# A PSUM bank for slot 7 and a place for the sixth pair of output tiles, in a fused sliding-window attention and MLP kernel

## The chip, the cores and the metric

The kernel runs on one core of one Trainium2 chip. The metric is the device time of one execution in microseconds, as the median of several executions. One program computes both stages; it holds most of its intermediate values on the chip and writes only the final output to memory.

## The reference, cut to what matters

Attention with a window of 32 positions to either side, on 8 batches of 8 heads, 576 positions and 64 elements per head. Its output, laid out as 4608 tokens of 512 elements, goes through a two-layer product with the piecewise quadratic activation SMeLU between the layers.

```python
def _attn_ref(q, k, v):                      # (8, 8, 576, 64) each
    scores = scale * np.matmul(q, k.transpose(0, 1, 3, 2))
    mask = np.abs(pos[:, None] - pos[None, :]) <= window      # window = 32
    scores = np.where(mask, scores, -1000000000.0)
    ...                                      # softmax over the last axis
    return np.matmul(attn, v)

def _moe_ref(x, w_in, w_out):                # x (4608, 512), w_in (512, 2048), w_out (2048, 512)
    h = x @ w_in
    g = np.where(h >= 1, h, np.where(h <= -1, 0.0, (h + 1) ** 2 / 4))
    return g @ w_out
```

## The kernel before, in the parts that matter

The second stage sets the rhythm. The tokens are taken in 18 blocks of 256 (TB), the hidden width of 2048 in 8 parts of 256 (NF). One *slot* `a` computes one part of one block: `t, f = divmod(a, 8)`. Slots 0 to 7 are block 0, slots 8 to 15 block 1, and so on. A slot does the following, in this order on each engine (the order of the text is the order of the instructions, engine by engine[...]):

```python
    for a in range(NF * NB + NF):
        t, f = divmod(a, NF)
        eng = None if a < 14 else V
        post = [x for n, x in pairs if n == a] + [a - NF] * (a >= 2 * NF + 2)
        # ... loads
        if a == 0 or a > 3:
            flush()                          # VectorE: xT <- attention output (L305, L308)
        if t < NB:
            # ... gT[t]
            r0 = TB * t % RING
            if a in (6, 7):
                hp = ps_o.tile([128, 2, TB], FP, name="hp", tag="op")
            else:
                hp = ps_h.tile([128, 2, TB], FP, name="hp", tag="hp")
            for j in range(2):
                for n, kk in enumerate((0, 2, 1, 3)):
                    nc.tensor.matmul(hp[:, j], w_in[:, kk, ...], xT[:, kk, r0:r0 + TB],   # L492, 8 of them
                                     start=n == 0, stop=n == 3)
            rr = ewp.tile([128, 2, TB], FP, name="rr")
            A.activation(rr, hp, AF.Relu, scale=0.5, bias=0.5)                           # L496
            g = gT[t][:, 2 * f:2 * f + 2]
            mx = ewp.tile([128, 2, TB], FP, name="mx")
            if a in two_on_act:              # (1, 7, 8, 9, 10, 11, 12)
                A.activation(mx, rr, AF.Square)                                          # L500
                V.scalar_tensor_tensor(g, hp, 1.0, mx, op0=ALU.max, op1=ALU.min)         # L501, reads hp
            else:
                V.tensor_max(mx, hp, rr)                                                 # L503, reads hp
                V.scalar_tensor_tensor(g, rr, 1.0, mx, op0=ALU.min, op1=ALU.mult)        # L504
        flush()
        run(a)                               # attention work placed at slot a
        for x in post:
            (pair if x < 4 * 4 else quarter)(x)      # second product: L448 in a pair, L432 in a quarter
        run(a + 0.5)                         # attention work placed after the second product
        # ... transposing loads
```

PSUM pools: `ps_h` gives the tiles `hp`, one bank each, and has two of them; `ps_o` gives the output tiles `op`, one bank each, and has two as well. A pool hands its banks out in turn, and a matmul that starts a new tile waits until the readers of the tile before it in that bank are done.

```python
    ps_h = ctx.enter_context(tc.tile_pool(name="ps_h", bufs=2, space=bass.MemoryType.PSUM))
    # ... ps_s and ps_n: one tile of two banks each, for scores, sums and transposes
    ps_o = ctx.enter_context(tc.tile_pool(name="ps_o", bufs=2, space=bass.MemoryType.PSUM))
```

In `ps_o` the order of tiles is: two small score tiles (slot 2), `hp` of slot 6, the output tile of block 0's first half (pairs 0 to 3), `hp` of slot 7, the output tile of block 1's first half (pairs 4 to 7), and then output tiles alone.

A *pair* is a quarter of the second product of one block for one half of the output columns, eight matmuls; it needs four parts of `gT` and half of the columns of four row blocks of `w_out`:

```python
    pairs = [(6, 0), (8, 1), (9, 2), (10, 3), (11, 4), (13, 5), (15, 6), (15, 8), (16, 7), (17, 9)]   # (slot, pair)

    def pair(x):
        half, p, g = x // 8, x % 8 // 4, x % 4       # half of the columns, block, group of four j
        # ... op[half, p] from ps_o at its first use
        for tt in range(2):
            for j in range(4 * g, 4 * g + 4):
                nc.tensor.matmul(o[:, tt], gT[p][:, j, ...], w_out[:, j, 256 * half:256 * half + 256], ...)   # L448
        # ... after the fourth: A.copy(osb, o) and a store of 256 rows
```

The attention work that stands near by:

```python
    at(3, (scores, 0, (1, 2), (0, 2), (2, 4), ps_n), (sums, 0, 0, TB, MAIN, ps_s))
    at(4, (sums, 0, 1, TB, MAIN))
    at(5, (sums, 0, 0, MAIN, S, ps_s))               # the last part of batch 0's attention, for slot 8's xT
    at(11, (tposes, 1, (0, 0), (0, 1)))              # batch 1: q transposed on TensorE (L187), copied to qT (L190)
    at(12, (tposes, 1, (1, 0), (1, 1)))              # batch 1: k likewise, to kT; written in the source as a loop
    at(13, seq[0][1])                                # batch 1: scores (bias L206, product L227, exp L235)
    at(13.5, (*seq[1][1], ps_n))                     # batch 1: scores, second part
    at(14, (*seq[0][0], ps_s), seq[1][0])            # batch 1: sums (L293), for slot 16's xT
```

Of the kernel before, what the change touches and what calls it, by code (L numbers as in the profile page):

```python
# [14 lines left out]
def kernel(  # L15
# [78 lines left out]
    def load_nat(b, t):  # L94
        src, dst, nm = ((q, qn, "qn"), (k, kn, "kn"))[t]
        x = dst[b] = nat.tile([128, NU, 2, D], BF, name=nm, tag=nm)
        for h in range(2):
            nc.gpsimd.dma_start(out=x[:, :, h], in_=src[b, NY * h:NY * h + NY].rearrange("y s d -> (y s) d")  # L98
                                .rearrange("(u p) d -> p u d", p=128))

    def load_v(b, n):
        if b not in vn:
            vn[b] = nat.tile([128, 2 * NC, 2, D], BF, name="vn", tag="vn", bufs=3)
        h, a = divmod(n, 2)
        y = NY * h + 2 * a
        nc.gpsimd.dma_start(out=vn[b][64 * a:64 * a + 64, :, h], in_=v[b, y:y + 2].rearrange("y s d -> (y s) d")  # L106
                            .rearrange("(c r) d -> r c d", r=64))
# [84 lines left out]
    def xpose(b, t):  # L192

        nc.sync.dma_start_transpose(out=qkT(b, t).rearrange("d (u p) -> d u p", p=128),
                                    in_=(qn, kn)[t][b].rearrange("p u h d -> p (u h d)"))
# [115 lines left out]
    def flush():  # L311
        while muls:
            muls.pop(0)()
# [61 lines left out]

    NB = NT // TB
    NF = DFF // 256
    pairs = [(6, 0), (8, 1), (9, 2), (10, 3), (11, 4), (13, 5), (15, 6), (15, 8), (16, 7), (17, 9)]
    two_on_act = (1, 7, 8, 9, 10, 11, 12)
    ev = {}  # L380

# [34 lines left out]
    for b in range(LONG, B):  # L416
        a = sl[5 * (b - 1) - 7] - 17
# [39 lines left out]
    def run(pos):  # L457
        todo = []
        for fn, *x in ev.get(pos, []):
            if fn is sums:  # L460
                todo.append(sums(*x))
            elif fn is tposes:
                tposes(*x)
            else:
                pool = (x.pop(),) if x[-1] in (ps_s, ps_n, ps_o) else ()
                fn(*x, eng, *pool)
        for end in todo:
            end()
# [5 lines that stand above are left out]
        for b, x in loads.get(a, []):  # L474
            if x < 2:
                load_nat(b, x)
            else:
                for n in range(4):
                    load_v(b, n)
# [3 lines that stand above are left out]
            if t not in gT:  # L483
                gT[t] = gtp.tile([128, 2 * NF, TB], BF, name="gT", tag="gT")
            r0 = TB * t % RING
            if a in (6, 7):
                hp = ps_o.tile([128, 2, TB], FP, name="hp", tag="op")
            else:
                hp = ps_h.tile([128, 2, TB], FP, name="hp", tag="hp")
            for j in range(2):  # L490
                for n, kk in enumerate((0, 2, 1, 3)):
                    nc.tensor.matmul(hp[:, j], w_in[:, kk, 256 * f + 128 * j:256 * f + 128 * j + 128],  # L492
                                     xT[:, kk, r0:r0 + TB], start=n == 0, stop=n == 3)
# [5 lines that stand above are left out]
            if a in two_on_act:  # L499
                A.activation(mx, rr, AF.Square)  # L500
                V.scalar_tensor_tensor(g, hp, 1.0, mx, op0=ALU.max, op1=ALU.min)  # L501
            else:
                V.tensor_max(mx, hp, rr)  # L503
                V.scalar_tensor_tensor(g, rr, 1.0, mx, op0=ALU.min, op1=ALU.mult)  # L504
        flush()
        run(a)
        for x in post:
            (pair if x < 4 * 4 else quarter)(x)
        run(a + 0.5)
        for x in xps.get(a, []):  # L510
            xpose(*x)
# [30 lines left out]
```

The softmax here doesn't subtract the row's maximum and nothing guards it: scores larger than these inputs give would overflow.

## Time and profile before

| | |
|---|---|
| time, median of 3 executions | 313.86 us (313.83 to 314.38) |
| the profiled execution | 313.74 us, of which 311.6 us are the span from the first to the last instruction |
| TensorE (PE) busy | 297.6 us, 95% of the span |
| VectorE (DVE) busy | 244.9 us, 79% |
| ScalarE (ACT) busy | 195.3 us, 63% |
| software DMA queue (GpSimd's loads) | 75.5% of the time of 16 DMA engines |

How to read it. Every instruction of the trace has a start in microseconds from the span's start, a duration, and, where its engine sat idle before it, the length of that idle time and the instruction that ended it (the releaser). The views used here are the page's first and fourth parts (busy time by engine; the chain of work that ended last), the list of waits of one engine, and the timeline of one engine in a window. A timeline merges equal instructions that follow each other and puts their number behind an x; the second column is then the time from the first one's start to the last one's end. Successive matmuls overlap, so the ends of neighbouring rows overlap too; the distance between two starts tells what one group costs. In the timeline of TensorE, L492 is a slot's first product, L448 a pair, L187 a transpose, L206 and L227 the bias and the product of a score tile, L293 the sums of attention and L432 a quarter of the second product for one tile of 128 tokens.

### The profile page before, as it was taken

How to read it: one execution, taken by the hardware profiler on the slowest of the kernel's cores; microseconds unless marked ns; L12 is line 12 of the kernel's file. 1: busy time of each engine (PE TensorE's matmuls, PEld its weight loads, DVE VectorE, ACT ScalarE, POOL GpSimd, SP SyncE). 2: the span in 40 equal slices, each digit the busy share in tenths (PEclk: the TensorE clock that was granted, in tenths of full speed). 3: DMA queues.
4: the chain of work that ended last, by engine and by line, in shares of the span. 5: the costliest groups of instructions: out<-in, count | busy, mean ns of one | idle time of the engine just before them, and what ended most of it. 6: DMA issues, size and time to landing. Idle time of an engine off the chain costs nothing.

```text
span 311.6 us, 8569 instructions
## 1 busy us (share of the span) xinstructions
PE 297.6 (95%) x3669; PEld 207.2 (66%) x3706; DVE 244.9 (79%) x381; ACT 195.3 (63%) x323; POOL 73.5 (24%) x89
## 2 busy tenths in 40 slices
PE   8997989999999999999999999999999999999995
PEld 3566868886666666666666666666666666666652
DVE  4287558888888888888888888888888888888760
ACT  3686876776765766567656666566676666554431
POOL 8898344643061223040504000000000000000000
PEclk9999999999999999999999999999999999999999
DMA  9999999999999999597998592005501100110111
GB/s 151 183 198 199 175 214 177 173 164 167 168 176 131 112 187 162 62 112 153 160 95 81 65 154 70 34 36 113 111 34 36 37 34 36 37 36 34 52 51 67
DMA packets 124118, 34.54 MB, mean 111 GB/s; under 512 B 108208, under 2 KB 119728, under 8 KB 124080
## 3 DMA queue, kind: packets, MB, share of 16 engines
q0 software_dynamic: 94736, 18.06, 75.5%
q1 hardware_dynamic: 29200, 15.63, 20.9%
q8 instruction: 29, 0.48, 0.6%
q10 hardware_dynamic: 144, 0.29, 0.3%
q14 instruction: 9, 0.07, 0.1%
HBM read 36.70 MB, written 9.44 MB: 148 GB/s over the span
## 4 chain that ended last, share of the span: by engine, by line
PE 91%; DVE 3%; ACT 3%; issue 3%; ACTq 0%
PE hp L492 39%; PE op L432 35%; PE bb L293 6%; PE op L448 4%; PE bb L227 2%; PE z L336 2%; PE tp L187 1%; DVE kT L190 1%; DVE xT L305 1%; ACT rc L300 1%; DVE mx L503 1%; ACT rr L496 1%; ACT lr L299 1%; DVE gT L501 0%; ACT mx L500 0%
## 5 line engine op out<-in xcount | busy, mean ns | idle before, releaser
L492 PE MATMUL hp<-xT,w_in 128*128 128x256 bf16 x1152 | 149.3, 273 | 2.8 <-DVE mx L503 1.9
L496 ACT ACTIVATE rr<-hp 128x512 f32<-128x512 f32 x144 | 85.7, 595 | 88.3 <-PE hp L492 88.2
L492 PEld LDWEIGHTS <-w_in 128*128 128x128 bf16 x1152 | 111.9, 98 | 42.5 <-issue 3.3
L432 PE MATMUL op<-w_out,gT 128*128 128x512 bf16 x477 | 123.0, 379 | 5.1 <-issue 4.9
L503 DVE TENSOR_TENSOR mx<-hp,rr 128x512 f32<-128x512 f32 x137 | 94.5, 690 | 31.8 <-ACT rr L496 29.6
L504 DVE SCALAR_TENSOR_TENSOR gT<-rr,mx 128x512 bf16<-128x512 f32 x137 | 95.3, 696 | 4.7
L432 PEld LDWEIGHTS <-gT 128*128 128x128 bf16 x512 | 47.5, 98 | 36.8
L235 ACT ACTIVATE pt<-bb 128x1024 bf16<-128x1024 f32 (+1 forms) x33 | 32.8, 1002 | 5.3 <-PE bb L227 3.8
L106 POOL DMA_DIRECT2D vn<-in_v_dram x32 | 27.3, 868 | 34.1 <-PE bb L227 31.5
L305 DVE TENSOR_TENSOR xT<-bb,rc 128x512 bf16<-128x512 f32 (+1 forms) x32 | 21.1, 658 | 10.1 <-ACT rc L300 9.6
L437 ACT COPY osb<-op 128x512 f32<-128x512 f32 x32 | 18.6, 583 | 11.5 <-PE op L432 11.1
L300 ACT ACTIVATE rc<-lr 128x512 f32<-128x512 f32 (+2 forms) x40 | 23.5, 587 | 1.3
L98 POOL DMA_DIRECT2D qn<-in_q_dram x10 | 12.2, 1221 | 43.5 <-DMA qT<-qn 37.5
L299 ACT ACTIVATE lr<-bb 128x512 f32<-128x512 f32 (+2 forms) x40 | 22.0, 551 | 0.2 <-PE bb L293 0.2
L201 DVE TENSOR_TENSOR pt<-pt,mask 128x1024 bf16<-128x1024 bf16 (+1 forms) x33 | 20.3, 614 | 0.0
L293 PE MATMUL bb<-pt,ones 64*64 64x256 bf16 (+3 forms) x352 | 19.5, 255 | 0.1
L293 PE MATMUL bb<-pt,vn 64*64 64x128 bf16 (+3 forms) x712 | 18.4, 204 | 0.0
L293 PEld LDWEIGHTS <-vn 64*64 64x64 bf16 x712 | 16.7, 107 | 0.2 <-DMA vn<-in_v_dram 0.2
L448 PE MATMUL op<-w_out,gT 128*128 128x256 bf16 x128 | 16.5, 273 | 0.0
L293 PEld LDWEIGHTS <-ones 64*64 64x64 bf16 x352 | 10.2, 105 | 8.5 <-issue 8.4
L98 POOL DMA_DIRECT2D kn<-in_k_dram x10 | 12.1, 1213 | 10.7 <-DMA kT<-kn 3.9
L227 PE MATMUL bb<-qT,kT 64*64 64x128 bf16 (+1 forms) x520 | 13.1, 217 | 0.4 <-DVE kT L190 0.4
(56 smaller groups left out, 118.7 us busy)
## 6 DMA issues: line engine op xcount, KB each, us to landing
out_dram<-osb SPq DMA_DIRECT2D x36, 256.0 KB, 2.3
vn<-in_v_dram POOLq DMA_DIRECT2D x32, 144.0 KB, 8.8
qn<-in_q_dram POOLq DMA_DIRECT2D x10, 288.0 KB, 7.2
kn<-in_k_dram POOLq DMA_DIRECT2D x10, 288.0 KB, 8.0
w_in<-in_moe_w_in_dram POOLq DMA_DIRECT2D x12, 128.0 KB, 5.6
w_out<-in_moe_w_out_dram POOLq DMA_DIRECT2D x3, 512.0 KB, 15.5
qn<-in_q_dram POOLq DMA_DIRECT2D x2, 576.0 KB, 12.8
kn<-in_k_dram POOLq DMA_DIRECT2D x2, 576.0 KB, 13.9
```

The costliest lines, as they stand in the source:

```text
L98: nc.gpsimd.dma_start(out=x[:, :, h], in_=src[b, NY * h:NY * h + NY].rearrange("y s d -> (y s) d") .rearrange("(u p) d -> p u d", p=128))
L106: nc.gpsimd.dma_start(out=vn[b][64 * a:64 * a + 64, :, h], in_=v[b, y:y + 2].rearrange("y s d -> (y s) d") .rearrange("(c r) d -> r c d", ...
L235: A.activation(p, ps[:, :, :w * n].rearrange(like, y=m), AF.Exp, scale=D ** -0.5)
L293: nc.tensor.matmul(bb[HD[h], a, o + c0:o + c1], ones[HD[a]] if c is None else vn[b][HD[a], c, h], p(a, h), start=n == 0, stop=True, skip_g ...
L299: A.activation(lr[:, :, :D0], bb[:, :, D0:2 * D0], AF.Ln)
L300: A.activation(rc[:, :, :D0], lr[:, :, :D0], AF.Exp, scale=-1.0)
L432: nc.tensor.matmul(o, gT[tt // 2][:, j, 128 * (tt % 2):128 * (tt % 2) + 128], w_out[:, j], start=not done, stop=len(done) == 2 * NF - 1, s ...
L448: nc.tensor.matmul(o[:, tt], gT[p][:, j, 128 * tt:128 * tt + 128], w_out[:, j, 256 * half:256 * half + 256], start=not done, stop=len(done ...
L492: nc.tensor.matmul(hp[:, j], w_in[:, kk, 256 * f + 128 * j:256 * f + 128 * j + 128], xT[:, kk, r0:r0 + TB], start=n == 0, stop=n == 3)
L496: A.activation(rr, hp, AF.Relu, scale=0.5, bias=0.5)
L503: V.tensor_max(mx, hp, rr)
L504: V.scalar_tensor_tensor(g, rr, 1.0, mx, op0=ALU.min, op1=ALU.mult)
```

## The change

Two edits. Slot 7's `hp` is taken from `ps_h` as in most slots, and only slot 6's comes from `ps_o`. Pair 5 (block 1, first half of the columns, parts 2 and 3 of block 1's `gT`, made in slots 10 and 11) is done in slot 12, after that slot's transposes of k, and no longer in slot 13, after the first score tile of batch 1. The first edit is for the bank in which slot 7's product lands, the second for what TensorE has to do while the transposed k is copied out of PSUM. Nothing else is added or removed: TensorE has the same instructions before and after, and eight weight loads with their eight matmuls stand earlier in its order (behind slot 12's transposes, ahead of slot 13's w_in product). The other engines keep their order.

```diff
@@ -375,7 +375,7 @@
 
     NB = NT // TB
     NF = DFF // 256
-    pairs = [(6, 0), (8, 1), (9, 2), (10, 3), (11, 4), (13, 5), (15, 6), (15, 8), (16, 7), (17, 9)]
+    pairs = [(6, 0), (8, 1), (9, 2), (10, 3), (11, 4), (12, 5), (15, 6), (15, 8), (16, 7), (17, 9)]
     two_on_act = (1, 7, 8, 9, 10, 11, 12)
     ev = {}
 
@@ -483,7 +483,7 @@
             if t not in gT:
                 gT[t] = gtp.tile([128, 2 * NF, TB], BF, name="gT", tag="gT")
             r0 = TB * t % RING
-            if a in (6, 7):
+            if a == 6:
                 hp = ps_o.tile([128, 2, TB], FP, name="hp", tag="op")
             else:
                 hp = ps_h.tile([128, 2, TB], FP, name="hp", tag="hp")
```

## The prediction

> **What bounds the kernel now.** I read the page's first and fourth parts first. From the page:
>
> ```profile
> PE 297.6 (95%) x3669; PEld 207.2 (66%) x3706; DVE 244.9 (79%) x381; ACT 195.3 (63%) x323; POOL 73.5 (24%) x89
> ...
> PE 91%; DVE 3%; ACT 3%; issue 3%; ACTq 0%
> ```
>
> TensorE is busy for 95% of the span and carries 91% of the chain that ended last. So a microsecond in which TensorE stands still is a microsecond of the total, unless it comes back as another wait. The edits touch no amount of work, so the question is which idle times of TensorE they can reach. The list of TensorE's waits (total us, times, longest us) has these rows:
>
> ```profile
> PE hp L492 <- DVE mx L503: 1.9, 1, 1.9
> PE bb L206 <- DVE kT L190: 0.6, 1, 0.6
> PE bb L227 <- DVE kT L190: 0.4, 2, 0.2
> ```
>
> One wait of 1.9 us, a w_in product behind the VectorE maximum of another slot, and short waits of batch 1's score tile behind the copies of the transposed k. TensorE's timeline places them:
>
> ```profile
> 26.07 1.04 PE L448 MATMUL op<-w_out,gT 128*128 128x256 bf16 x8
> 29.01 1.91 PE L492 MATMUL hp<-xT,w_in 128*128 128x256 bf16 x16 [1.91 <-DVE mx L503]
> 30.76 1.04 PE L448 MATMUL op<-w_out,gT 128*128 128x256 bf16 x8
> 31.63 1.04 PE L492 MATMUL hp<-xT,w_in 128*128 128x256 bf16 x8
> ...
> 39.07 1.20 PE L187 MATMUL tp<-ident,kn 128*64 128x128 bf16 x36
> 40.20 1.05 PE L492 MATMUL hp<-xT,w_in 128*128 128x256 bf16 x8
> 41.90 0.41 PE L206 MATMUL bb<-bias,ident 64*64 64x512 bf16 x4 [0.65 <-DVE kT L190]
> 42.11 0.24 PE L227 MATMUL bb<-qT,kT 64*64 64x128 bf16 x2
> 42.53 0.41 PE L227 MATMUL bb<-qT,kT 64*64 64x128 bf16 x14 [0.18 <-DVE kT L190]
> 42.88 1.05 PE L448 MATMUL op<-w_out,gT 128*128 128x256 bf16 x8
> 43.85 0.41 PE L206 MATMUL bb<-bias,ident 64*64 64x512 bf16 x4
> ```
>
> Row 1 is slot 6's pair 0; row 2 is slot 7's and slot 8's products in one piece (16 matmuls) with the 1.91 us ahead of slot 7; rows 3 and 4 are slot 8's pair 1 and slot 9. Below the cut come slot 12's transposes of k, slot 13's product, the score tile with its two waits (0.65 + 0.18 = 0.83 us), pair 5, and the second score tile. VectorE's timeline shows what it does meanwhile:
>
> ```profile
> 27.20 0.69 DVE L504 SCALAR_TENSOR_TENSOR gT<-rr,mx 128x512 bf16<-128x512 f32 x1
> 27.81 0.55 DVE L308 TENSOR_TENSOR xT<-bb,rc 128x384 bf16<-128x384 f32 x1
> 28.28 0.68 DVE L503 TENSOR_TENSOR mx<-hp,rr 128x512 f32<-128x512 f32 x1
> 29.00 0.69 DVE L504 SCALAR_TENSOR_TENSOR gT<-rr,mx 128x512 bf16<-128x512 f32 x1
> 31.38 0.69 DVE L501 SCALAR_TENSOR_TENSOR gT<-hp,mx 128x512 bf16<-128x512 f32 x1 [1.69 <-ACT mx L500]
> ```
>
> The maximum at 28.28 is slot 6's; it ends at 28.96 and slot 7 starts at 29.01. Slot 7 waits because its tile has the bank of slot 6's tile. The row above it, L308, is the last piece of batch 0's attention output, which slot 8 needs: it ends at 28.36.
>
> **What the Trainium skill says.** "TensorE: Matmul & The Clock Gate", What overlaps and what doesn't (in The mechanism): matmuls start and end strictly in program order. The trace agrees: in the 1.91 us nothing else runs on TensorE. The same page, Back-to-back issue gap, gives 262 cycles at 2.4 GHz for 256 columns, that is 109 ns; here 30.76 to 31.63 is 0.87 us for eight, 109 ns each, so I count 0.87 us for a w_in product or a pair. "Perfetto Trace Analysis", Matmuls, says that independent groups should rotate through different PSUM banks so that the emptying of one lies beside the next group's matmuls; slot 7 in slot 6's bank shows the contrary. "DMA: Bandwidth & Descriptors", Issuing engines are not separate DMA queues, says that transfers of all issuers interleave on the same engines; that bears on a rival below.
>
> **Part one, slot 7's bank.** In ps_h slot 7 follows slots 4 and 5, so it gets slot 4's bank, whose last reader (the L503 at 24.63) ended at 25.31: free.
> - Slot 7 can start when pair 0 has been issued, 26.07 + 0.87 = 26.94. Its weights were there: the last two w_in loads landed 7.4 us after issues at 18.5 and 19.1, by 26.5.
> - Slot 8 would follow at 27.81, but needs L308, 28.36, plus 0.04 of handoff: 28.40. So a new wait of 0.6 us takes part of the gain. Its bank, slot 5's, is free at 26.49 + 0.68 = 27.17.
> - Pair 1 at 28.40 + 0.87 = 29.27, before 30.76: 1.49 us earlier.
> - Slot 9 now comes into slot 7's bank, whose last reader is slot 7's L501. Slot 7's ScalarE work (0.60 and 0.63) is done at about 29.25, but VectorE is in L504 until 29.69; L501 runs 29.61 to 30.30. Slot 9 could start at 30.14 and starts at 30.34, before 31.63: 1.29 us earlier. Slot 10 needs slot 8's L501, done at about 31.45, and comes at 32.08: no wait.
>
> From there to the transposes every dependency hangs on the w_in product of the same or the preceding slot, so 1.29 us should hold: transposes of k at 37.78 in place of 39.07.
>
> **Part two, pair 5.** The kT copies hang on slot 12's product through ScalarE and VectorE and end at 42.48 before, so about 41.20 after. TensorE after the transposes (37.78 + 1.13 = 38.91): pair 5 with the change of shape 0.98 (as 42.88 to 43.85), slot 13 to about 40.76, the bias matmuls about 0.2, then the product waits for the copies until 41.24; 0.2 to 0.3 us of the 0.83 stay. The product takes 0.41 to its end; the second score tile's bias starts at about 41.66, before 43.85: 2.19 us earlier.
>
> Then ScalarE holds it back a little. The first exponential started at 42.99, 0.05 after its product; it would start at 41.70. The next can follow after about 0.91 (spacing of 20.14 to 21.06 elsewhere in ScalarE's timeline), at 42.61, before 44.54: 1.93 us earlier. ScalarE ran without a gap from there to slot 16's xT: the second multiplication (L305) ended at 49.00 and slot 16, begun at 48.88, needs it at its third matmul, 49.10. That leaves no slack, so 1.93 us is what gets through. Behind slot 16 TensorE had only short issue gaps (4.9 us over 31 times in the L432 groups, all 0.2 us or less), which don't change. Sum: 313.86 - 1.93 = 311.93, called 311.9.
>
> **The rivals.**
> 1. *Both waits vanish whole*: 1.91 + 0.83 = 2.74, 311.1 us. Against it are L308 at 28.36, and ScalarE's unbroken row from 44.54.
> 2. *The loads take over.* Batch 1's q and k were issued at 23.64 and 24.38 and landed 9.7 and 11.9 us later, at 33.3 and 36.3; the transposes that use them would start at 34.8 and 37.8, 1.5 us behind each. The store of block 0's first half (256 KB, issued at 36.21) would go out at 34.9 and share the engines with k's load; at some 200 GB/s it moves in 1.3 us, and should delay k by less than that. If k came at 38.5 or later, 0.7 us or more of part one would be lost: about 312.7. Similarly the second half of w_out lands at 28.49 + 15.5 = 44.0, and pair 8 would use it at 46.1 in place of 48.0.
> 3. *The ring gets too short.* Slots 7, 8 and 9 now share two banks while VectorE is late with slot 6. If slot 7's L501 slipped by a whole operation (0.69), slot 9 would start at about 31.0, and the gain of part one falls to 0.6; total about 312.6. For worse than before, slot 9 would have to start after 31.63, and nothing on VectorE or ScalarE reaches that far.
> 4. *TensorE runs ahead into a later stage's limit.* VectorE is at 79%; in the later windows the loads have long landed, and I see no other engine that would pull the end back to its old place.
>
> **Range and chances.** Rival 1 sets the low end, 311.1; rivals 2 and 3 the high end, with a little for the spread of the three times before (0.55 us): 313.0. Gaining 2% would take 6.3 us, more than all TensorE waits named here; losing 2% would need a stall that nothing shows. Faster by over 2%: 0.01; within 2%: 0.98; slower: 0.01.
>
> **What would show it.** Right, if TensorE's timeline has slot 7 at about 26.9, slot 8 at 28.4 with a wait put down to L308 (xT), slot 9 near 30.3 with a short wait for L501, transposes of k near 37.8, pair 5 directly behind, a remaining kT wait of at most 0.3, and slot 16 near 47.0. Wrong, if slot 8 starts at 27.8 (then L308 doesn't bind), if the transposes wait for a load, or if the starts behind slot 16 are less than 1.5 us earlier than before.

## The result, and the profile after

| | before | changed |
|---|---|---|
| time, median | 313.87 us (313.83 to 314.38) | 311.78 us (311.61 to 312.14) |
| ratio, with its 95% interval | | 0.9931 (0.9914 to 0.9948) |
| span of the profiled execution | 311.6 us | 310.0 us |

The changed kernel is 2.09 us shorter (0.7%). Two later comparisons gave it 311.93 us (ratio 0.9937, 0.9925 to 0.9949) and 312.34 us (0.9952, 0.9938 to 0.9965); the median of its 15 single times is 311.98. The prediction was 311.9, by way of a gain of 1.93 us.

From the page of the changed kernel, the busy times and the chain that ended last:

```profile
PE 296.7 (96%) x3669; PEld 206.7 (67%) x3706; DVE 244.7 (79%) x381; ACT 195.3 (63%) x323; POOL 73.8 (24%) x89
...
PE 88%; DMA 4%; POOL 3%; issue 2%; ACT 1%; DVE 0%; POOLq 0%
```

The busy times are within 1 us of those of before. In the chain VectorE has gone from 3% to nothing, and loads have come in with 4%: the first sign of what the removed wait had stood in front of. TensorE's waits in the changed kernel (total us, times, longest us), the rows that answer to those of before:

```profile
PE hp L492 <- DMA w_in<-in_moe_w_in_dram: 1.1, 2, 0.6
...
PE bb L227 <- DVE kT L190: 0.2, 1, 0.2
PE hp L492 <- DVE gT L501: 0.2, 1, 0.2
```

The wait of 1.9 us for L503 and the one of L206 are gone; the remaining L227 row is slot 2's. New are 0.2 us for L501, as the ring of two banks would have it, and 0.6 us more of waiting for w_in. TensorE's timeline of the changed kernel:

```profile
26.78 1.04 PE L448 MATMUL op<-w_out,gT 128*128 128x256 bf16 x8
27.65 2.02 PE L492 MATMUL hp<-xT,w_in 128*128 128x256 bf16 x16
29.51 1.04 PE L448 MATMUL op<-w_out,gT 128*128 128x256 bf16 x8
30.77 1.03 PE L492 MATMUL hp<-xT,w_in 128*128 128x256 bf16 x8 [0.22 <-DVE gT L501]
...
38.23 1.20 PE L187 MATMUL tp<-ident,kn 128*64 128x128 bf16 x36
39.36 1.05 PE L448 MATMUL op<-w_out,gT 128*128 128x256 bf16 x8
...
41.45 0.66 PE L227 MATMUL bb<-qT,kT 64*64 64x128 bf16 x16
41.90 0.43 PE L206 MATMUL bb<-bias,ident 64*64 64x512 bf16 x4
```

Slot 7 follows pair 0 at once (26.78 + 0.87 = 27.65), and pair 5 fills the place behind the transposes. The row of slots 7 and 8 is 2.02 us long where 1.91 would do: slot 8 waits 0.11 us for L308, and no gap is printed. The L227 row is 0.66 us long where 0.41 would do: some 0.2 us of the kT wait are left, hidden inside a merged row (by starts, 41.45 to 41.90 is 0.45 us, and the same step takes 0.22 to 0.24 without a wait: 8.53 to 8.75 and 19.67 to 19.91 in the trace of before). Slot 9's wait is printed as 0.22 us, counted from the modelled end of the row before it; by starts it is 30.77 - 29.51 - 0.87 = 0.39. The distance of starts is the safer reading wherever rows overlap.

In this execution pair 0 comes 0.71 us later than before (26.78, not 26.07): 0.22 us because slot 0 started later (14.81, not 14.59), the rest because slot 4 waited for its weights. VectorE, which has the chain, is only 0.23 us later:

```profile
28.04 0.55 DVE L308 TENSOR_TENSOR xT<-bb,rc 128x384 bf16<-128x384 f32 x1
...
29.22 0.69 DVE L504 SCALAR_TENSOR_TENSOR gT<-rr,mx 128x512 bf16<-128x512 f32 x1
30.02 0.69 DVE L501 SCALAR_TENSOR_TENSOR gT<-hp,mx 128x512 bf16<-128x512 f32 x1
```

Slot 16 starts at 47.26 in place of 48.88, which is 1.62 us earlier, and from slot 17 to the end the two traces keep a distance of 1.56 to 1.57 us.

### The profile page after: what moved, and what is told of

It is laid out like the page before. It is cut to its first block, busy times and chain, and to the rows that moved or that the text cites. A ratio compares the mean times of both kernels' runs of the same rounds, so it can differ in the third digit from the quotient of the medians.

```text
span 310.0 us, 8569 instructions
## 1 busy us (share of the span) xinstructions
PE 296.7 (96%) x3669; PEld 206.7 (67%) x3706; DVE 244.7 (79%) x381; ACT 195.3 (63%) x323; POOL 73.8 (24%) x89
## 4 chain that ended last, share of the span: by engine, by line
PE 88%; DMA 4%; POOL 3%; issue 2%; ACT 1%; DVE 0%; POOLq 0%
PE hp L492 39%; PE op L432 35%; PE bb L293 6%; PE op L448 4%; DMA w_in<-in_moe_w_in_dram 4%; PE bb L227 2%; PE tp L187 1%; POOL vn L106 1%; POOL w_in L110 1%; ACT pt L235 1%; POOL kh L85 0%; DVE gT L501 0%; ACT mx L500 0%; PE bb L252 0%; ACT rr L496 0%
## 5 line engine op out<-in xcount | busy, mean ns | idle before, releaser
L432 PE MATMUL op<-w_out,gT 128*128 128x512 bf16 x477 | 123.0, 379 | 5.1 <-issue 4.9
L503 DVE TENSOR_TENSOR mx<-hp,rr 128x512 f32<-128x512 f32 x137 | 94.5, 690 | 31.1 <-ACT rr L496 29.0
L504 DVE SCALAR_TENSOR_TENSOR gT<-rr,mx 128x512 bf16<-128x512 f32 x137 | 95.2, 695 | 4.7
L432 PEld LDWEIGHTS <-gT 128*128 128x128 bf16 x512 | 47.5, 98 | 36.8
L227 PE MATMUL bb<-qT,kT 64*64 64x128 bf16 (+1 forms) x520 | 13.1, 217 | 0.3 <-DVE kT L190 0.2
```

The lines of the kernel that those rows point to most:

```text
L432: nc.tensor.matmul(o, gT[tt // 2][:, j, 128 * (tt % 2):128 * (tt % 2) + 128], w_out[:, j], start=not done, stop=len(done) == 2 * NF - 1, s ...
```

## The experiments

All times are medians with the range of single times; ratios are to the kernel before, with 95% intervals. Besides the times I compare two distances within one trace, which don't depend on when the first loads came: from the first product of slot 0 to batch 1's transposes of k (part one), and from these to slot 16 (part two). Before, slot 0's product (its first matmul behind the first xT) starts at 14.59, the transposes at 39.07 and slot 16 at 48.88: 24.48 and 9.81 us. The first row, from TensorE's timeline of before:

```profile
14.59 1.69 PE L492 MATMUL hp<-xT,w_in 128*128 128x256 bf16 x14 [0.43 <-DVE xT L305]
```

**e1_bank_only: slot 7's bank alone**

```diff
-    pairs = [..., (11, 4), (12, 5), ...]
+    pairs = [..., (11, 4), (13, 5), ...]        # against the changed kernel
```

> Only slot 7's bank is changed; pair 5 stays in slot 13. The chain theory (slot 8 waits for L308, slot 9 for slot 7's L501) gives 1.3 us less than before, about 312.6, with the score tile's waits for kT left at about 0.8 us in the list of waits. The rival that the wait of 1.9 us vanishes whole gives 312.0. The rival that the loads of batch 1 hold the transposes gives 313 or more, with an idle time ahead of L187 put down to a load.

Measured: 312.96 us (312.28 to 313.65), ratio 0.9974 (0.9967 to 0.9982). The trace is that of the shortest execution. Its TensorE timeline:

```profile
14.47 1.69 PE L492 MATMUL hp<-xT,w_in 128*128 128x256 bf16 x14 [0.43 <-DVE xT L305]
...
27.01 1.04 PE L492 MATMUL hp<-xT,w_in 128*128 128x256 bf16 x8
28.29 1.03 PE L492 MATMUL hp<-xT,w_in 128*128 128x256 bf16 x8 [0.24 <-DVE xT L308]
29.16 1.04 PE L448 MATMUL op<-w_out,gT 128*128 128x256 bf16 x8
30.21 1.03 PE L492 MATMUL hp<-xT,w_in 128*128 128x256 bf16 x8
...
37.65 1.20 PE L187 MATMUL tp<-ident,kn 128*64 128x128 bf16 x36
...
40.47 0.41 PE L206 MATMUL bb<-bias,ident 64*64 64x512 bf16 x4 [0.64 <-DVE kT L190]
```

Slot 8 waits for L308 and slot 9 comes 0.18 us behind the end of pair 1's issue (30.21 - 29.16 - 0.87): both new waits are there. Transposes of k at 37.65 less slot 0 at 14.47 is 23.18, so part one is worth 24.48 - 23.18 = 1.30 us, against 1.29 predicted, and the kT wait is untouched. The rival "all of 1.9 us" falls, and so does the one that the loads hold the transposes. But the median gained only 0.91 us, and single times spread over 1.4 us: e9 and e10 took that up.

**e2_pair_only: pair 5 alone**

```diff
-            if a == 6:
+            if a in (6, 7):                     # against the changed kernel
```

> Only pair 5 is moved to slot 12; slot 7 keeps slot 6's bank. The chain theory: the copies of kT end as late as before, the second score tile comes 0.9 us earlier, and ScalarE's row of two exponentials lets 0.64 us of it through to slot 16: about 313.2. The rival without a limit from ScalarE gives 313.0 (0.83 to 0.9 us). The rival that this part is worth nothing alone, because slot 16 hangs on ScalarE, gives 313.8. The wait of 1.9 us of L492 for L503 stays.

Measured: 313.03 us (312.71 to 313.55), ratio 0.9973 (0.9964 to 0.9981). The profiled execution is the longest, with late loads. In its timeline slot 7 still waits for slot 6's L503, but only 1.28 us:

```profile
27.28 1.04 PE L448 MATMUL op<-w_out,gT 128*128 128x256 bf16 x8
29.60 1.91 PE L492 MATMUL hp<-xT,w_in 128*128 128x256 bf16 x16 [1.28 <-DVE mx L503]
```

Pair 0 is 1.21 us later than in the trace of before (27.28, not 26.07), slot 7 only 0.59 us (29.60, not 29.01): the old wait swallows 0.62 us of lateness. Transposes to slot 16: 48.68 - 39.66 = 9.02, so part two is worth 0.79 us at the start of slot 16, and 0.73 us at slot 17 (50.94 - 39.66, against 51.08 - 39.07 before). That lies between the theory with ScalarE (0.64) and the one without (0.83 to 0.9), and the median of 0.84 doesn't tell them apart; e6 does. That this part is worth nothing alone has fallen.

**e6_half_exponential: less for ScalarE between the score tiles and slot 16**

```diff
-        A.activation(p, ps[...].rearrange(like, y=m), AF.Exp, scale=D ** -0.5)
+        hs = slice(0, 1 if b == 1 and pool is ps_n else 2)
+        A.activation(p[:, hs], ps[...].rearrange(like, y=m)[:, hs], AF.Exp, scale=D ** -0.5)
```

Half of that exponential is left out; ones stand in its place, written by a VectorE memset in slot 9.

> As the changed kernel, but the exponential of batch 1's second score tile (slot 13.5) takes one half of the tile; the other half is left out and holds ones, written by VectorE in slot 9. If ScalarE's row limits part two, the second sums of slot 14 start without the gap of 0.3 us and slot 16 comes 0.3 us earlier against the score tiles: 311.5. If TensorE alone sets it, nothing changes: 311.8.

Measured: 312.13 us (311.86 to 312.54), ratio 0.9940 (0.9928 to 0.9952), so no gain in the median; the changed kernel beside it had 311.93. The trace says why. The last row of slot 14's first sums and the first of the second ones, in the changed kernel and here, from TensorE's timelines:

```profile
43.76 0.26 PE L293 MATMUL bb<-pt,vn 64*64 64x128 bf16 x8
44.14 0.29 PE L293 MATMUL bb<-pt,ones 64*64 64x224 bf16 x4
```

```profile
44.08 0.26 PE L293 MATMUL bb<-pt,vn 64*64 64x128 bf16 x8
44.16 0.27 PE L293 MATMUL bb<-pt,ones 64*64 64x224 bf16 x4
```

The step is 0.38 us in the changed kernel and 0.08 with the shorter exponential: ScalarE's two exponentials in a row do hold the second sums, by 0.30 us. Transposes to slot 16 is 47.26 - 38.55 = 8.71, where the changed kernel has 9.03 (47.26 - 38.23). So the limit is real: from the transposes to slot 17 this run is 1.10 us shorter than the kernel before (51.08 - 39.07 less 49.46 - 38.55), the changed kernel 0.72. In this execution slot 4 waited 0.90 us for w_in, which put the transposes at 38.55, and the total hides the 0.3 us. Five executions with loads that vary like this can't resolve it.

**e7_changed_l308_early: is L308 the limit?**

```diff
-                V.scalar_tensor_tensor(g, rr, 1.0, mx, ...)      # L504
+                # slot 5's L504 is put off until slot 6's flush (L308) is issued
+                (late.append if a == 5 else lambda f: f())(lambda ...: V.scalar_tensor_tensor(g, rr, 1.0, mx, ...))
-            flush()
+            flush(); [late.pop()() for _ in late[:]]
```

> The changed kernel with L308 ahead of slot 5's L504 on VectorE. If slot 8's wait for L308 costs 0.6 us by itself, the time falls to about 311.3. If slot 9's wait for slot 7's L501 stands right behind it, slot 8 comes earlier, slot 9 does not, and the time stays at 311.8.

Measured: 312.05 us (311.60 to 312.36), ratio 0.9934 (0.9922 to 0.9946): nothing against the changed kernel's 311.93. Its timeline:

```profile
27.66 1.91 PE L492 MATMUL hp<-xT,w_in 128*128 128x256 bf16 x16
29.40 1.04 PE L448 MATMUL op<-w_out,gT 128*128 128x256 bf16 x8
30.77 1.03 PE L492 MATMUL hp<-xT,w_in 128*128 128x256 bf16 x8 [0.33 <-DVE gT L501]
```

Slot 8 follows slot 7 without a gap, and slot 9 waits 0.50 us by starts (30.77 - 29.40 - 0.87) for slot 7's L501. What slot 8 wins, slot 9 waits away: in the first trace of the changed kernel slot 7 started at 27.65 too, L308 held slot 8 by 0.11 us, and slot 9 came at the same 30.77. In this execution loads were late too, so the trace doesn't show by how much L308 would have bound.

**e3_six_inside: the other slot in the output bank**

```diff
-            if a == 6:
+            if a == 7:
```

> As the changed kernel, but slot 7 takes the output bank and slot 6 one of the usual two. If slot 9's wait for slot 7's L501 is what the ring of two banks costs, it goes away: slot 9 starts straight behind pair 1, 0.2 to 0.4 us earlier against slot 8 than in the changed kernel, and the time is about 311.5. If L308 alone holds this stretch, slot 9 keeps its place and the time stays at 311.8. Slot 6 may wait about 0.15 us for slot 4's L503.

Measured: 311.56 us (311.51 to 312.15), ratio 0.9934 (0.9922 to 0.9947); by the intervals not to be told from the changed kernel. In its timeline slot 9's wait is gone:

```profile
29.64 1.04 PE L448 MATMUL op<-w_out,gT 128*128 128x256 bf16 x8
30.51 1.04 PE L492 MATMUL hp<-xT,w_in 128*128 128x256 bf16 x8
31.60 1.03 PE L448 MATMUL op<-w_out,gT 128*128 128x256 bf16 x8
```

30.51 is 29.64 + 0.87. But pair 2 starts 0.22 us later than it could (31.38): it needs the third load of w_out, which landed at 31.56 in this execution (issued at 22.9, 8.7 us to landing). So the loads do come next in line, at pair 2 and not at the transposes, where rival 2 of the prediction had looked for them.

**e4_six_inside_l308_early: both waits taken away**

The edits of e3 and e7 together.

> As e3_six_inside, and VectorE does L308 ahead of slot 5's L504 instead of behind it, so that xT is there 0.64 us earlier. If L308 is what holds slot 8, slots 8 and 9 come 0.4 us earlier than in e3_six_inside and the time is about 311.2. If the loads are next in line (the part of w_out for pair 2, or batch 1's k), idle time ahead of L448 or L187 is put down to a load and the time stays at 311.5.

Measured: 311.46 us (311.07 to 312.22), ratio 0.9930 (0.9918 to 0.9943). The trace is of the shortest execution, with loads on time:

```profile
27.09 1.91 PE L492 MATMUL hp<-xT,w_in 128*128 128x256 bf16 x16
28.84 1.04 PE L448 MATMUL op<-w_out,gT 128*128 128x256 bf16 x8
29.71 1.04 PE L492 MATMUL hp<-xT,w_in 128*128 128x256 bf16 x8
30.59 1.04 PE L448 MATMUL op<-w_out,gT 128*128 128x256 bf16 x8
```

Slots 7, 8, pair 1, slot 9 and pair 2 follow each other at 0.87 us. Transposes of k at 37.15 less slot 0 at 14.54 is 22.61: 1.87 us for part one, nearly the whole 1.91. So L308 and slot 7's L501 together are what had cut part one to 1.30.

**e8_w_in_split: smaller loads for slots 4 and 5**

```diff
-    w += [(load_w_in, 1024, 1536, h) for h in range(2)]
+    w += [(load_w_in, c, c + 256, h) for c in range(1024, 1536, 256) for h in range(2)]
     # and the two slices of w that are issued end at 14, not 12
```

> The changed kernel with the w_in loads for slots 4 and 5 (two of 256 KB read in bf16 terms) as four loads of half the size, slot 4's first. If late loads of w_in decide single executions, slot 4's wait for w_in goes away, the spread narrows and the median falls by 0.2 to 0.5 us, to 311.4. If they don't matter, the time stays at 311.8; the two more loads to be issued may bring later loads 0.5 us behind.

Measured: 312.71 us (311.78 to 313.35), ratio 0.9954 (0.9940 to 0.9969): no gain, a miss. That it is slower than the changed kernel is not shown: that had 311.93 us beside it, but the intervals overlap, and in e12 the changed kernel itself has 0.9952. From its timeline, slot 4 and pair 2:

```profile
22.58 1.05 PE L492 MATMUL hp<-xT,w_in 128*128 128x256 bf16 x8
...
32.25 1.03 PE L448 MATMUL op<-w_out,gT 128*128 128x256 bf16 x8 [0.43 <-DMA w_out<-in_moe_w_out_dram]
```

Slot 4 no longer waits, as hoped, but the third load of w_out is issued at 24.4 (22.5 in the trace of e5 below) and lands at 32.2 (30.5 there), so pair 2 waits instead. Not all of that comes from the two more loads: the fourth load of w_in had landed at 14.94 here and at 13.55 in e5. In e6, where it landed as late (14.74), the third load of w_out is issued at 23.3 and lands at 31.7, so some 0.5 us are left for the split. In this execution the lateness was moved and not taken away.

**e9 and e10: where e1's long executions lose their time**

The kernel of e1 twice more.

> The kernel of e1_bank_only once more, for the trace of another execution. Its times went from 312.28 to 313.65, and the trace of the first is that of the shortest. The lateness theory: in a longer execution a load for slots 2 to 5 or for pair 2 lands later than in the first, TensorE waits for it, and the time is longer by about the shift of slot 16. The rival: the loads land as before and the time is lost elsewhere, behind slot 16.

> As e9_bank_only_second: a third execution of the same kernel; the two theories expect the same of it.

Measured: 312.42 and 313.06 us. The second of the two weight loads for slots 4 and 5 landed at 21.88 in e1's trace, at 22.00 in e9's and at 22.43 in e10's, and the times are 312.28, 312.42 and 313.06. In e10's timeline:

```profile
22.56 1.03 PE L492 MATMUL hp<-xT,w_in 128*128 128x256 bf16 x8 [0.42 <-DMA w_in<-in_moe_w_in_dram]
...
24.96 0.81 PE L492 MATMUL hp<-xT,w_in 128*128 128x256 bf16 x6 [0.51 <-issue]
```

Slot 4 waits for its weights, and slot 5 stops in its middle (what for the trace doesn't say); slot 16 is 0.78 us later than in e1's trace (48.23, not 47.45), as the whole time is (313.06 - 312.28 = 0.78). All of it is there by the transposes of k (38.43, not 37.65) and nothing is lost behind slot 16, so the rival falls. Slot 4's start makes 0.55 of the 0.78 us (22.56, not 22.01), so in e10 most of the time is lost where the lateness theory says. In e9 it is not: slot 4 found its weights (it starts at 22.15), and the 0.14 us are about those by which slot 0 started later (14.60, not 14.47).

**e5 and e12: the changed kernel twice more**

> The changed kernel as it is, with more executions. The chain theory gives 311.9 for every execution, with a spread like that of the kernel before (0.8 us). The lateness theory says that the wait of 1.9 us in the kernel before also took up loads of w_in that come up to 1.2 us late in some executions: then single times lie between 311.4 and 312.6, the median near 311.8, and the executions with a longer wait of L492 for w_in are the longer ones.

> The changed kernel, for the comparison with e11 on one chip: 311.9.

Measured: 311.93 us (311.61 to 312.47) and 312.34 us (311.82 to 312.69). The two traces are of executions of 311.87 and 311.82 us, in which slot 4 found its weights. TensorE's timeline of e5:

```profile
14.80 1.69 PE L492 MATMUL hp<-xT,w_in 128*128 128x256 bf16 x14 [0.43 <-DVE xT L305]
...
27.14 1.04 PE L492 MATMUL hp<-xT,w_in 128*128 128x256 bf16 x8
28.62 1.03 PE L492 MATMUL hp<-xT,w_in 128*128 128x256 bf16 x8 [0.44 <-DVE xT L308]
29.49 1.04 PE L448 MATMUL op<-w_out,gT 128*128 128x256 bf16 x8
30.54 1.03 PE L492 MATMUL hp<-xT,w_in 128*128 128x256 bf16 x8
...
37.98 1.20 PE L187 MATMUL tp<-ident,kn 128*64 128x128 bf16 x36
```

Slot 0 started at 14.80 here, 0.21 us later than before. Less that, slot 8 is at 28.41, slot 9 at 30.33 and the transposes of k at 37.77; the prediction had 28.40, 30.34 and 37.78. In the first trace of the changed kernel (312.14 us) slot 4 waited 0.58 us for w_in and the transposes came 0.25 us later. Lateness of that load thus decides a few tenths of a microsecond between executions; that it explains the whole spread was not shown.

**e11_six_inside_l308_early_again: the best version beside the changed kernel**

> The kernel of e4 beside the changed kernel on one chip. Where loads are on time it was 1.1 us shorter than the changed kernel in their traces (0.8 after the different start); late loads take part of that back: 0.3 to 0.8 us less than e12, about 311.3. The rival that late loads eat all of it gives the time of e12.

Measured on the same chip as e12: 311.38 us (311.31 to 311.49), ratio 0.9920 (0.9907 to 0.9934), against e12's 0.9952 (0.9938 to 0.9965). The intervals don't meet: this version is 0.96 us shorter than the changed kernel there and 2.4 us shorter than the kernel before, although slot 4 waited 0.49 us for w_in in its trace. Somewhat more than the 0.3 to 0.8 us expected; e12's median is the highest of the three of the changed kernel.

## Why the prediction was right, point by point

- **Part one, slot 7's bank.** Predicted 1.29 us; 1.30 in e1's trace and in e5's (24.48 less 37.98 - 14.80), 1.29 in e12's and 1.06 in the first changed trace, where slot 4 waited 0.58 us for its weights. Its inner steps held as well: slot 7 straight behind pair 0, slot 8 held by L308, slot 9 by slot 7's L501. e4 shows that these two are the cause of the lost 0.6 us, as it gets 1.87 without them; e3 and e7 show that slot 9's wait alone can be taken away, and that earlier xT alone brings nothing while that wait stands.
- **Part two, pair 5.** Predicted 0.64 us. Measured 0.78 at the start of slot 16 (9.81 less 9.03), but 0.72 at slot 17 (51.08 - 39.07 less 49.52 - 38.23), and this is what stays: slot 16 now waits for its xT inside its own row (1.08 us long, 1.04 before), which its start doesn't show. TensorE's timeline before and of the changed kernel:

```profile
44.42 1.05 PE L492 MATMUL hp<-xT,w_in 128*128 128x256 bf16 x8
...
48.88 1.04 PE L492 MATMUL hp<-xT,w_in 128*128 128x256 bf16 x8
...
51.08 1.04 PE L492 MATMUL hp<-xT,w_in 128*128 128x256 bf16 x8
```

```profile
47.26 1.08 PE L492 MATMUL hp<-xT,w_in 128*128 128x256 bf16 x8
...
49.52 1.04 PE L492 MATMUL hp<-xT,w_in 128*128 128x256 bf16 x8
```

The mechanism was right: a kT wait of some 0.2 us stays, and e6 shows the limit from ScalarE. The spacing of the two exponentials was right too, 0.92 us (43.07 - 42.15) for a predicted 0.91. ScalarE's timeline before, of the changed kernel, and of the changed kernel in a window that begins behind the first exponential:

```profile
44.54 1.02 ACT L235 ACTIVATE pt<-bb 128x1024 bf16<-128x1024 f32 x1 [0.53 <-PE bb L227]
45.50 0.60 ACT L496 ACTIVATE rr<-hp 128x512 f32<-128x512 f32 x1
```

```profile
42.15 1.94 ACT L235 ACTIVATE pt<-bb 128x1024 bf16<-128x1024 f32 x2 [0.24 <-PE bb L227]
```

```profile
43.07 1.02 ACT L235 ACTIVATE pt<-bb 128x1024 bf16<-128x1024 f32 x1
43.98 0.60 ACT L496 ACTIVATE rr<-hp 128x512 f32<-128x512 f32 x1
```

Of the 0.08 us by which the prediction fell short, 0.05 are slack behind the second exponential, which it took as none. Before, the relu of slot 14 started 0.96 us behind it, at the end of slot 14's product (44.42 + 1.05 = 45.47); now it starts 0.91 behind it. The last 0.03 us are not traced to one step. A larger slip had no effect: the prediction let the first score tile's product cost the 0.41 us of its row, where the distance of starts is 0.22 to 0.24. The second score tile thus came 1.11 us earlier against the transposes (43.85 - 39.07 less 41.90 - 38.23), not 0.90, but ScalarE holds what follows; e6 gets 1.10 with a shorter exponential.
- **The sum.** In e5's trace, with timely loads, slot 17 comes 2.04 us earlier against slot 0 (51.08 - 14.59 less 49.25 - 14.80), of which part one makes 1.30; the medians of the three comparisons gained 1.44 to 2.09. The median of the changed kernel's 15 single times gives 313.87 - 311.98 = 1.89. The 1.93 came out so near in part by luck: the sum was set 0.1 us too small, while late loads, which I had not counted, take a similar amount back in the median.
- **Rival 1**, both waits whole (2.74), is refuted by e1 and e5. e4's kernel comes near it, with 2.60 us at slot 17 (36.49, slot 0 to slot 17 before, less 48.43 - 14.54).
- **Rival 2**, loads that take over at the transposes: no trace shows a wait there. In the first changed trace the k load lands at 37.73 and is used at 38.23, so 0.5 us were left of the 1.5 expected; in e5 it lands at 36.25 and is used at 37.98. Loads do bind elsewhere, at slot 4 and at pair 2 (e3, e8), which the prediction did not name.
- **Rival 3**, the short ring: the wait exists, 0.18 us with timely loads and 0.39 to 0.50 where slot 7 was late, as slot 7's L501 then waits for ScalarE (30.02 in the changed trace, behind L504's end at 29.91).
- **Rival 4**, a later limit: none shows, as the distance between the traces stays at 1.56 to 1.57 us from slot 17 to the end (the last w_in product starts at 299.22 and 297.65). The 31 short issue gaps in the L432 groups (4.9 us), which the prediction counts there, are not idle time: that page has 3669 matmuls for 3706 weight loads, and the four traces with 3706 of both (e9 to e12) have no such gaps.

## What to carry to other kernels

When a wait is removed, write down what each next instruction on the engine needs and when that is ready: here the second and third in line took back 0.6 of 1.9 us, and a list of ready times from the old trace gave their starts to 0.01 us. A wait on a busy engine is also a buffer: it swallows late loads, and without it the same lateness shows in the time, so expect a larger spread (0.8 us over 25 executions of the kernel before, 1.4 over 15 of e1's) and compare more executions. Distances between two events within one trace separate the effect of a change from the lateness ahead of it.

## What the runs showed of the hardware

The same load, issued at the same place of the program, landed at quite different times from one execution to the next: the second weight load for slots 4 and 5 at 21.73 us in e5, at 21.84 before, at 22.87 in the first changed trace and at 23.37 in e2. Part of that is a later issue (15.32, 15.43, 15.80 and 16.20 us); from issue to landing it took 6.4, 6.4, 7.1 and 7.2 us.

The issue itself hangs on older loads. In all 14 traces GpSimd issued no load sooner than 0.28 us after the load eight places before it had landed, and some twenty loads of each trace at just that distance. So the eighth load of w_in was issued at 13.69 us before and at 14.60 in the first changed trace, because the fourth (four loads of q and k lie between) had landed at 13.41 and at 14.31. What sets the eight is not shown.

Two additional loads in the issuing order (e8) brought a load that came later to its landing some 0.5 us later than in e6, an execution with loads about as late from the start, although the bytes were the same.
